# Heads in pairs of nine token slots, and attention in a fixed order among groups of four MLP matmuls

## Chip, cores, metric

The kernel runs on one core of a Trainium2 chip. The metric is the device time of one execution in microseconds (us). A ratio is the record's ratio of fast runs, with its 95% interval; it is not quite the ratio of the medians that are quoted beside it.

Engine names in the profile: PE is TensorE's matmuls, PEld its weight loads, DVE is VectorE, ACT is ScalarE, POOL is GpSimd, SP is SyncE. The granted clock is TensorE's clock as the profile records it, as a share of full speed.

## The reference

Linear ("performer") attention over 64 heads, then an MLP over all 4608 tokens:

```python
# q, k, v: (8, 8, 576, 64); omega: (128, 64)
q_s, k_s = q * scale, k * scale                  # scale = 1 / 64**0.25
phi(x) = exp(x @ omega.T - |x|^2/2 - max(...)) / sqrt(128)
q_p, k_p = phi(q_s), phi(k_s)                    # (8, 8, 576, 128)
kv  = einsum('bhsm,bhsd->bhmd', k_p, v);  z = sum(k_p, axis=s)
out = (q_p @ kv) / (q_p @ z + 1e-6)              # (8, 8, 576, 64)
x = out.transpose(0, 2, 1, 3).reshape(4608, 512)
h = x @ w_in                                     # 512 -> 2048
y = (h * sigmoid(1.702 * h)) @ w_out             # 2048 -> 512
```

The sigmoid is computed as `0.5 * (1 + tanh(0.851 h))`, and the factor 0.5 is applied at the end.

## The kernel before

One head at a time: q and k are transposed together (`qkTp`), projected (`pq`, `pk`), exponentiated on ScalarE, the key maximum is folded into v on VectorE (`maxE`, `emax`, `vp`), `kv` and the numerator and denominator (`nk`) follow, and the quotient goes to `xb`. After eight heads `xb` is transposed into `xt`. The MLP runs over blocks of 512 tokens. The attention is recorded with high priority, and a scheduler decides the order on each engine.

```python
    ps_h = ctx.enter_context(tc.tile_pool(name="ps_h", bufs=2, space=PSUM))   # two rotating buffers
    ps_o = ctx.enter_context(tc.tile_pool(name="ps_o", bufs=1, space=PSUM))
    ...
    def moe_block(tok0, ntok):
        gT = gtp.tile([128, NFC, TOK_BLK], BF16, name="gT", tag="gT")
        for f in range(NFC):                                  # 16 groups of 128 hidden units
            ph = ps_h.tile([128, TOK_BLK], F32, name="ph", tag="ph")
            for c in range(CM):                               # four matmuls: a "first-layer quantum"
                nc.tensor.matmul(ph[:, 0:ntok], lhsT=win[:, c, ...], rhs=xt[c][...],
                                 start=(c == 0), stop=(c == CM - 1))
            th = thp.tile([128, TOK_BLK], BF16, name="th", tag="th")
            nc.scalar.activation(out=th[...], in_=ph[...], func=AF.Tanh, scale=0.851)
            nc.vector.scalar_tensor_tensor(out=gT[:, f, ...], in0=th[...], scalar=1.0,
                                           in1=ph[...], op0=ALU.add, op1=ALU.mult)
        for r0 in range(0, ntok, 128):
            po = ps_o.tile([128, DM], F32, name="po", tag="po")
            for f in range(NFC):                              # 16 matmuls: second layer
                nc.tensor.matmul(po[0:m, :], lhsT=gT[:, f, r0:r0+m], rhs=wout[:, f, :], ...)
            ... osb = 0.5 * po on ScalarE, then stored ...
    ...
    for b in range(B):
        with tc.high_priority(offset=2_000_000):
            for h in range(H):
                attention_head(b, h, xb)
                ...
            xb_to_xt(b, xb)
        ... moe_block for every block whose tokens are there ...
```

The softmax here doesn't subtract the row's maximum and nothing guards it: scores larger than these inputs give would overflow.

## Time and profile before

| | before |
|---|---|
| time, median of 2 | 433.59 us |
| TensorE busy | 86% |
| VectorE busy | 64% |
| DMA packets under 512 B | 124,032 of 132,778 |

The page of the kernel before. First the busy time of each engine with its share of the span and its number of instructions; then, from the strip of 40 equal slices, TensorE and its granted clock in tenths and the DMA share; then the chain of work that ended last, by engine and by line.

```profile
PE 372.1 (86%) x2801; PEld 189.3 (44%) x2801; DVE 276.9 (64%) x787; ACT 208.5 (48%) x454; POOL 139.3 (32%) x345
...
PE   0066597889988899989999899989999999999895
...
PEclk9999999999999999999999999999999999999999
DMA  9999589579799479669879759101101001011011
...
PE 33%; ACT 5%; DVE 4%; issue 1%; DVEq 0%; ACTq 0%
PE po L260 18%; PE ph L237 12%; DVE gT L248 3%; ACT th L245 3%; ACT osb L268 1%; ACT qeT L160 1%; PE qkTp L152 1%; PE nk L200 1%; PE xps L222 0%; PE pq L159 0%; PE nk L188 0%; DVE vp L178 0%; ACT ke L172 0%; DVE xb L209 0%; PE pk L166 0%
```

The reader sees a slow start, then TensorE close to full at full clock to the end. DMA is busy, at first full (share 1.11 in the first 60 us, 0.84 from 80 to 200 us), until shortly before the attention ends at 286 us.

The windows table of the kernel before: per stretch the busy time of each engine with the number of instructions, the granted clock, the DMA share, and GB/s.

```profile
80.00:200.00 120.00, 110.50 (x1005) 58.47 (x1003) 102.92 (x321) 71.26 (x162) 57.80 (x142) 1.00 0.84 93
285.00:420.00 135.00, 129.34 (x613) 57.07 (x612) 49.43 (x88) 51.72 (x95) 0.00 (x0) 1.00 0.10 37
```

While attention runs, VectorE and TensorE are both nearly always busy. In the second line only the MLP is left, but for the last copies of attention up to 286 us, and TensorE is busy 129 of 135 us.

The wait list of the kernel before: who waited for whom, us in total, how often, the longest.

```profile
PE ph L237 <- DVE gT L248: 6.6, 19, 1.4
```

The timeline of the kernel before in that last stage (start, duration, engine, line, what; in brackets the idle time of the engine before it and what ended it). It shows two first-layer quanta in flight:

```profile
397.40 0.38 PE L237 MATMUL ph<-xt_116,win 128*128 128x512 bf16 x1
...
398.27 0.38 PE L237 MATMUL ph<-xt_116,win 128*128 128x512 bf16 x1
398.46 0.60 ACT L245 ACTIVATE th<-ph 128x512 bf16<-128x512 f32 x1 [0.97 <-PE ph L237]
...
399.10 0.69 DVE L248 SCALAR_TENSOR_TENSOR gT<-th,ph 128x512 bf16<-128x512 bf16 x1 [0.88 <-ACT th L245]
...
399.83 0.38 PE L237 MATMUL ph<-xt_116,win 128*128 128x512 bf16 x1
```

A quantum starts at 397.40 and the next one at 398.27, while the first one's tanh (398.46) and gT (399.10) are still to come. The bank of the first (a bank is here one 128x512 float32 buffer of PSUM, the memory that the matmuls write to) is free again at 399.79, and the matmul at 399.83 takes it. So one bank cycles in 2.43 us and carries one quantum; two banks carry two quanta in 2.43 us.

### The profile page before, as it was taken

Reading aid. Unit: us, or ns where it says so; the run is one execution under the profiler, and the core shown is the slowest. Engines: PE = TensorE matmul, PEld = TensorE weight load, DVE = VectorE, ACT = ScalarE, POOL = GpSimd, SP = SyncE. Lnnn points to the kernel's source line nnn. Section 1 sums busy time; section 2 is a strip of 40 time slices with the busy share of each in tenths; the row PEclk is TensorE's granted clock in tenths of the full one; section 3 lists DMA queues with packets and bytes.
Section 4 is the critical chain, followed back from the end, with each engine's and each line's share of the span. In section 5 each row is a group of like instructions: output and inputs, shape, how many; then the busy total and the mean of one; then the engine's idle time right before and its main releaser. Section 6 shows DMA issues by size and latency. Waiting matters only on the chain. (4 is left out here: it accounts for less than half of the span.)

```text
span 431.9 us, 8223 instructions
## 1 busy us (share of the span) xinstructions
PE 372.1 (86%) x2801; PEld 189.3 (44%) x2801; DVE 276.9 (64%) x787; ACT 208.5 (48%) x454; POOL 139.3 (32%) x345
## 2 busy tenths in 40 slices
PE   0066597889988899989999899989999999999895
PEld 0044344454555454445455445444434444444342
DVE  1378769897799878889789878872351441523501
ACT  1044166565576545666467546633452433434412
POOL 8378256256266157256356336000000000000000
PEclk9999999999999999999999999999999999999999
DMA  9999589579799479669879759101101001011011
GB/s 163 248 257 174 63 67 103 66 73 139 120 80 97 70 85 143 93 54 124 130 79 101 81 74 133 38 2 49 50 0 73 27 24 74 1 49 38 7 67 37
DMA packets 132778, 36.21 MB, mean 84 GB/s; under 512 B 124032, under 2 KB 126080, under 8 KB 132736
## 3 DMA queue, kind: packets, MB, share of 16 engines
q0 software_dynamic: 86176, 12.58, 41.5%
q1 hardware_dynamic: 46560, 23.11, 19.4%
q8 instruction: 22, 0.36, 0.4%
q14 instruction: 20, 0.16, 0.1%
HBM read 38.80 MB, written 9.44 MB: 112 GB/s over the span
## 5 line engine op out<-in xcount | busy, mean ns | idle before, releaser
L260 PE MATMUL po<-wout,gT 128*128 128x512 bf16 (+1 forms) x592 | 163.5, 380 | 3.3 <-ACT osb L268 1.8
L248 DVE SCALAR_TENSOR_TENSOR gT<-th,ph 128x512 bf16<-128x512 bf16 (+2 forms) x160 | 99.2, 625 | 93.5 <-ACT th L245 92.8
L245 ACT ACTIVATE th<-ph 128x512 bf16<-128x512 f32 (+2 forms) x160 | 88.4, 555 | 69.1 <-PE ph L237 57.5
L237 PEld LDWEIGHTS <-win 128*128 128x128 bf16 x640 | 56.2, 98 | 58.2 <-issue 13.3
L124 POOL DMA_DIRECT2D qkh<-in_q_dram x63 | 54.7, 868 | 82.0 <-PE qkTp L152 69.6
L260 PEld LDWEIGHTS <-gT 128*128 128x128 bf16 (+1 forms) x592 | 53.7, 98 | 55.2 <-DVE gT L248 5.8
L160 ACT ACTIVATE qeT<-pq 128x512 bf16<-128x512 f32 (+1 forms) x128 | 49.2, 435 | 56.8 <-PE pq L159 43.9
L237 PE MATMUL ph<-xt_116,win 128*128 128x512 bf16 (+2 forms) x160 | 57.2, 360 | 8.4 <-DVE gT L248 6.6
L174 DVE TENSOR_REDUCE maxE<-ke 128x5 f32<-128x640 bf16 x64 | 52.1, 814 | 8.3 <-ACT ke L172 8.1
L237 PE MATMUL ph<-xt_117,win 128*128 128x512 bf16 (+2 forms) x160 | 57.3, 361 | 0.0
L237 PE MATMUL ph<-xt_118,win 128*128 128x512 bf16 (+2 forms) x160 | 57.0, 359 | 0.0
L237 PE MATMUL ph<-xt_119,win 128*128 128x512 bf16 (+2 forms) x160 | 57.0, 359 | 0.0
L128 POOL DMA_DIRECT2D qkh<-in_k_dram x63 | 54.8, 871 | 1.8 <-DMA qkh<-in_k_dram 0.8
L268 ACT ACTIVATE osb<-po 128x512 f32<-128x512 f32 (+1 forms) x37 | 22.1, 598 | 67.6 <-PE po L260 67.6
L159 PE MATMUL pq<-qkT,omT_106 64*128 64x512 bf16 (+1 forms) x128 | 31.8, 320 | 17.5 <-DVE qkT L154 17.3
L172 ACT ACTIVATE ke<-pk 128x640 bf16<-128x640 f32 x64 | 45.6, 712 | 0.3
L152 PE MATMUL qkTp<-ident,qkh 128*128 128x128 bf16 x320 | 31.2, 230 | 12.3 <-DMA qkh<-in_k_dram 5.9
L154 DVE COPY qkT<-qkTp 128x640 bf16<-128x640 bf16 x64 | 30.9, 483 | 12.7 <-PE qkTp L152 11.3
L152 PEld LDWEIGHTS <-qkh 128*128 128x128 bf16 x320 | 24.3, 102 | 33.0 <-issue 28.4
L178 DVE TENSOR_TENSOR vp<-vst,emax 128x325 bf16<-128x325 f32 x64 | 30.6, 478 | 1.4 <-DVE rden L208 0.4
L209 DVE TENSOR_TENSOR xb<-nk,rden 128x320 bf16<-128x320 f32 x64 | 31.0, 484 | 0.3
L166 PE MATMUL pk<-omT_106,qkT 64*128 64x128 bf16 x320 | 31.1, 230 | 0.0
(38 smaller groups left out, 263.1 us busy)
## 6 DMA issues: line engine op xcount, KB each, us to landing
out_dram<-osb SPq DMA_DIRECT2D x35, 256.0 KB, 2.0
vst<-in_v_dram SPq DMA_DIRECT2D x64, 128.0 KB, 2.7
qkh<-in_q_dram POOLq DMA_DIRECT2D x63, 80.0 KB, 3.1
qkh<-in_k_dram POOLq DMA_DIRECT2D x63, 80.0 KB, 3.4
wout_p<-in_moe_w_out_dram SPq DMA_DIRECT2D x16, 256.0 KB, 6.1
win<-in_moe_w_in_dram POOLq DMA_DIRECT2D x16, 128.0 KB, 6.6
vst<-in_v_dram SPq DMA_DIRECT2D x64, 16.0 KB, 2.7
out_dram<-osb SPq DMA_DIRECT2D x2, 128.0 KB, 2.3
```

The costliest lines, as they stand in the source:

```text
L124: nc.gpsimd.dma_start(qkh[:, :, 0:64], qrows[row0 : row0 + SPAD, :].rearrange("(t p) d -> p t d", p=128),)
L128: nc.gpsimd.dma_start(qkh[:, :, 64:128], krows[row0 : row0 + SPAD, :].rearrange("(t p) d -> p t d", p=128),)
L152: nc.tensor.transpose(qkTp[:, t * 128 : (t + 1) * 128], qkh[:, t, :], ident[:])
L159: nc.tensor.matmul(pq[:, 0:cn], lhsT=omT2[0:64, :], rhs=qkT[0:64, c0 : c0 + cn])
L160: nc.scalar.activation(out=qeT[:, c0 : c0 + cn], in_=pq[:, 0:cn], func=AF.Exp, scale=SCALE)
L166: nc.tensor.matmul(pk[:, t, :], lhsT=qkT[64:128, t * 128 : (t + 1) * 128], rhs=omT2[64:128, :],)
L172: nc.scalar.activation(out=ke[:], in_=pk[:], func=AF.Exp, scale=SCALE)
L174: nc.vector.reduce_max(out=maxE[:], in_=ke[:], axis=AX.X)
L237: nc.tensor.matmul(ph[:, 0:ntok], lhsT=win[:, c, f * 128 : (f + 1) * 128], rhs=xt[c][:, tok0 : tok0 + ntok], start=(c == 0), stop=(c == CM ...
L245: nc.scalar.activation(out=th[:, 0:ntok], in_=ph[:, 0:ntok], func=AF.Tanh, scale=0.851)
L248: nc.vector.scalar_tensor_tensor(out=gT[:, f, 0:ntok], in0=th[:, 0:ntok], scalar=1.0, in1=ph[:, 0:ntok], op0=ALU.add, op1=ALU.mult,)
L260: nc.tensor.matmul(po[0:m, :], lhsT=gT[:, f, r0 : r0 + m], rhs=wout[:, f, :], start=(f == 0), stop=(f == NFC - 1),)
```

## The change

Its intent: fewer and larger operations in attention, and a hand-made order that hides them in the MLP.

- Two heads at a time. Each partition holds nine neighbouring tokens of one head (64 partitions per head), read as one contiguous run of 2,304 bytes. Loads and keys are no longer padded to 640 tokens; the query side of the numerator and denominator still is.
- The projections of even and odd slots use the upper and lower half of TensorE's rows ("row-tiled", 64*128 in the trace, where a full one is 128*128), and so do the `kv` matmuls of the two heads.
- The scheduler is switched off. The MLP is cut into 288 quanta of four matmuls: the 16 first-layer quanta of a block, then its 16 second-layer quanta. Attention's steps are placed after fixed quanta, one pair per 8 quanta (per 5 at first). The first four pairs form a prologue.
- gT of a quantum is recorded one quantum late, after the tanh of the next.
- The PSUM buffers become single tiles made once. `ph` is one tile of two banks, used in turn.

```diff
-    ps_h = ctx.enter_context(tc.tile_pool(name="ps_h", bufs=2, space=bass.MemoryType.PSUM))
...
+    with tc.manual_schedule():
...
+        tr = psum.tile([128, 1024], BF16, name="tr")
+        pqk = psum.tile([128, 2, 512], F32, name="pqk")
+        nd = psum.tile([128, 2, 512], F32, name="nd")
+        ph = psum.tile([128, 2, 512], F32, name="ph")
+        po = psum.tile([128, 512], F32, name="po")
...
+        def K(i):                       # key projection of a pair, row-tiled by slot parity e
+            for j in range(4):
+                for e in range(2):
+                    nc.tensor.matmul(pqk[:, e, j*128:(j+1)*128],
+                                     lhsT=t[64*e:64*e+64, j, :], rhs=omT[64*e:64*e+64, :])
+            nc.tensor.matmul(nd[:, 0, 384:512], ...)     # the ninth slot goes to the nd tile
+            nc.tensor.matmul(nd[:, 1, 384:512], ...)
...
+        for i in range(9, npairs):
+            start[i] = start[8] + 8 * (i - 8)
...
+            at(s, t1); at(s + 1, t2); at(s + 2, kk); at(s + 3, ...); ...
...
+        hbanks = [ph[:, 0, :], ph[:, 1, :]]
+        for s, u in enumerate(quanta):
+            if u[0] == "a":                              # first layer
+                dst = hbanks[hb % 2]
+                hb += 1
+                m1(n, f, dst)
+                t = tanh(n, f, dst)
+                for p in pend:
+                    stt(*p)                              # gT of the quantum before
+                pend = [(n, f, t, dst)]
+            else:                                        # second layer
+                m2(n, r, g, po[:])
+                ...
+            for fn in items.pop(s, []):                  # attention steps of this place
+                fn()
```

(The diff is cut to its core and its long lines are shortened.)

## The prediction

> **What bounds it now.** Two stages. Up to 285 us attention runs, and VectorE with its waits bounds it: the windows table gives VectorE 103 of 120 us busy from 80 to 200 us (union; TensorE 110, ScalarE 71). In the timeline at 130-140 us a head takes 3.07 us, with VectorE issuing all the time and six MLP matmuls. From 285 us there is only MLP (TensorE 95%), and the chain of waits is 18% po, 12% ph. Before 57 us little MLP runs and DMA is full (share above 1.0) with 124,032 packets under 512 B.
>
> **What changes.** 32 pairs replace 64 heads, without padding 576 tokens to 640.
> - DMA: 2,304-byte runs in place of 256-byte ones. DMA stops limiting. [...] (share 0.10 for 39 GB/s of 2 KB output packets, 1.1 for 106 GB/s of small ones).
> - VectorE per pair: from the groups, 6.6 us (summed durations) to about 4.6 us: PSUM copy of 1024 about 0.68 (128 takes 0.215, 640 takes 0.483), max halves 0.45, reduce of 576 0.75, vp 0.75, xb 0.81, xt copy 0.45, reciprocals 0.37.
> - ScalarE per pair about equal (3.6 to 3.3 us).
> - TensorE attention about 2.3 us per pair. Row tiling gains little: pq and pk already overlap (135.08 and 135.09 us)[...].
> - MLP: 288 quanta of four matmuls at 0.864 us = 249 us. But order becomes static: a block's first-layer quanta, then its second-layer quanta. Filling ph waits with po goes.
>
> **Critical path, from trace durations.**
> 1. Prologue: four pairs in series, about 9 us each because VectorE and ScalarE are in order: first MLP quantum at about 43 us.
> 2. Block 0 (pairs every 5 quanta): about 49 us.
> 3. Blocks 1-6, a pair per 8 quanta. In first-layer stretches ph has two banks; a bank cycles in 2.43 us (chain: 1.04 matmul, 0.65 tanh, 0.70 gT), so 1.215 us a quantum at best. The large exponential ahead of tanh and the max group ahead of gT stretch 8 quanta with their pair to about 12 us. Second-layer stretches: 8 x 0.864 + 2.3 + po waits, about 10 us. Block: 44 us, six blocks: 264 us.
> 4. Blocks 7-8 without attention: 16 x 1.215 + 4 x 4.30 = 36.6 us each, 73 us.
> 5. Tail 3 us.
> Sum 432 us: most of the saved work turns into static-order waits. I lean lower: the prologue may be pessimistic.
>
> **Prediction: 429 us, range 405 to 450. Faster by over 2%: 0.42; within 2%: 0.36; slower: 0.22.**
>
> **What would show it.** TensorE busy below before's 86%; ph matmuls waiting over 50 us for gT (VectorE); tanh waiting behind exponentials; first MLP matmul at 38-48 us; last two blocks at 36 us each; VectorE busy about 210 us (union); DMA packets under 512 B nearly gone; block period near 44 us; po waiting 0.8 us for osb per output tile at the end.
>
> **What would make it wrong.** Faster: the prologue takes about 25 us, or attention's ScalarE and VectorE work fits between tanh and gT so that a first-layer pair takes 10 us: then about 400. Slower: [...] halved kv matmuls (18 of 65 columns) cost more than 0.03 us each, or late weights stall TensorE's fixed order: then 450 or more.

What no trace or run shows is cut out of it, and each cut is marked. The sum: 43 + 49 + 264 + 73 + 3 = 432 us. TensorE's 2.3 us for a pair is given without its parts and is to be read as an estimate; the other durations are read from the groups and timelines of the kernel before, or estimated from them.

## The result and the profile after

The changed kernel is correct and takes 633.07 us (629.63 and 636.51) against 433.59 us: ratio 1.4603, 95% interval 1.4413 to 1.4793. This is far outside the range of the prediction.

The page after, the same parts: busy time, then TensorE, granted clock and DMA by slices, then the chain, then three of the costliest groups (busy, mean ns of one, idle time of the engine before them and what ended it).

```profile
PE 426.2 (68%) x2834; PEld 195.6 (31%) x2881; DVE 228.1 (36%) x405; ACT 201.4 (32%) x409; POOL 40.6 (6%) x78
...
PE   3456668765886678668865885678658755765575
...
PEclk9999989977798799779978797799789955695569
DMA  9991114411142115111511130002000200020002
...
PE 57%; ACT 20%; DVE 17%; issue 4%; DMA 1%; another core or an unknown queue 1%; POOL 0%; ACTq 0%; DVEq 0%; POOLq 0%
PE ph L253 32%; PE po L273 18%; DVE gT L267 14%; ACT th L263 13%; ACT ke L141 3%; PE nd L215 2%; ACT osb L283 1%; PE pqk L130 1%; PE tr L106 1%; PE tr L238 1%; PE nd L197 1%; DMA qk<-in_q_dram 1%; PE pqk L152 1%; ACT kvs L209 1%; DVE vp L186 1%
...
L253 PE MATMUL ph<-xt,win 128*128 128x512 bf16 x553 | 200.4, 491 | 151.0 <-DVE gT L267 143.1
L267 DVE SCALAR_TENSOR_TENSOR gT<-th,ph 128x512 bf16<-128x512 bf16 x144 | 98.7, 687 | 265.6 <-ACT th L263 265.6
L263 ACT ACTIVATE th<-ph 128x512 bf16<-128x512 f32 x144 | 86.0, 597 | 266.7 <-PE ph L253 263.9
```

VectorE and ScalarE did get less work, and no engine is full. In the chain, ph, th and gT now stand with 32, 13 and 14%. The granted clock also falls, to about half in some slices near the end (0.51 from 501.49 to 540.76 us).

The wait list after, and a line of its windows table for a stretch that has first-layer quanta only (columns as before):

```profile
PE ph L253 <- DVE gT L267: 143.1, 125, 1.8
```

```profile
501.49:540.76 39.27, 22.20 (x48) 6.82 (x49) 8.25 (x12) 7.16 (x12) 0.00 (x0) 0.51 0.00 0
```

TensorE sat idle 143.1 us before first-layer matmuls, waiting for gT, where it had waited 6.6 us. In the stretch of 39.27 us, 12 quanta pass at a granted clock of 0.51, with TensorE busy 22.20 us, VectorE 8.25 and ScalarE 7.16: the three sums make about the whole stretch, which is what one chain through three engines looks like.

The timeline after in a stretch without attention, which is the same work as the stretch shown of before:

```profile
502.87 1.86 PE L253 MATMUL ph<-xt,win 128*128 128x512 bf16 x4 [1.41 <-DVE gT L267]
...
504.77 0.60 ACT L263 ACTIVATE th<-ph 128x512 bf16<-128x512 f32 x1 [2.68 <-PE ph L253]
505.40 0.69 DVE L267 SCALAR_TENSOR_TENSOR gT<-th,ph 128x512 bf16<-128x512 bf16 x1 [2.58 <-ACT th L263]
506.14 0.59 PE L253 MATMUL ph<-xt,win 128*128 128x512 bf16 x1 [1.41 <-DVE gT L267]
```

Matmuls, tanh, gT, matmuls: one at a time, with every engine idle while the two others work. One quantum takes 3.27 us. Two banks are there, but nothing overlaps. The four matmuls take 1.86 us where they took 1.02 us elsewhere (495.57 us, before the clock fell): TensorE also runs at half speed, at the granted clock of 0.51.

At first sight this chain looks impossible, since the next matmuls use the *other* bank. The start of the MLP shows which gT is meant. The timeline after of ScalarE and of VectorE there:

```profile
45.73 0.60 ACT L263 ACTIVATE th<-ph 128x512 bf16<-128x512 f32 x1 [4.97 <-PE ph L253]
48.28 0.60 ACT L263 ACTIVATE th<-ph 128x512 bf16<-128x512 f32 x1 [1.95 <-PE ph L253]
```

```profile
48.91 0.69 DVE L267 SCALAR_TENSOR_TENSOR gT<-th,ph 128x512 bf16<-128x512 bf16 x1 [4.54 <-ACT th L263]
```

The first gT needs the first tanh, which ended at 46.33. VectorE had been idle for 4.54 us, and still gT started only at 48.91, when the *second* tanh had ended. The waits in the built program say the same for quantum 124 of 144:

```
changed kernel:   gT #124 waits for tanh #125     matmuls of #126 wait for gT #124
two tiles (e3):   gT #124 waits for tanh #124     matmuls of #126 wait for gT #124
```

So the theory A that the experiments test: the recording layer treats the tile `ph` as one thing. When different engines use it, it puts all uses in the recorded order, whichever bank they touch. Recorded are matmuls(f), tanh(f), gT(f-1), matmuls(f+1), and that is how they run. The order holds between two *reads* too, and across the banks: tanh #125 and gT #124 read different banks, and gT #124 waits all the same; in the trace the first gT starts at 48.91 us, after the second tanh, and in the two-tile run at 46.37 us, after its own. The waits stand already in the program that the recording layer built; why it sets them is not shown.

### The profile page after: what moved, and what is told of

Read it like the earlier page. It is cut to its first block, busy times and chain, and to the rows that moved or that the text cites. A ratio compares the mean times of both kernels' runs of the same rounds, so it can differ in the third digit from the quotient of the medians.

```text
span 627.9 us, 7057 instructions
## 1 busy us (share of the span) xinstructions
PE 426.2 (68%) x2834; PEld 195.6 (31%) x2881; DVE 228.1 (36%) x405; ACT 201.4 (32%) x409; POOL 40.6 (6%) x78
## 4 chain that ended last, share of the span: by engine, by line
PE 57%; ACT 20%; DVE 17%; issue 4%; DMA 1%; another core or an unknown queue 1%; POOL 0%; ACTq 0%; DVEq 0%; POOLq 0%
PE ph L253 32%; PE po L273 18%; DVE gT L267 14%; ACT th L263 13%; ACT ke L141 3%; PE nd L215 2%; ACT osb L283 1%; PE pqk L130 1%; PE tr L106 1%; PE tr L238 1%; PE nd L197 1%; DMA qk<-in_q_dram 1%; PE pqk L152 1%; ACT kvs L209 1%; DVE vp L186 1%
## 5 line engine op out<-in xcount | busy, mean ns | idle before, releaser
L253 PE MATMUL ph<-xt,win 128*128 128x512 bf16 x553 | 200.4, 491 | 151.0 <-DVE gT L267 143.1
L267 DVE SCALAR_TENSOR_TENSOR gT<-th,ph 128x512 bf16<-128x512 bf16 x144 | 98.7, 687 | 265.6 <-ACT th L263 265.6
L263 ACT ACTIVATE th<-ph 128x512 bf16<-128x512 f32 x144 | 86.0, 597 | 266.7 <-PE ph L253 263.9
L273 PE MATMUL po<-wout,gT 128*128 128x512 bf16 x552 | 142.3, 389 | 8.9 <-ACT osb L283 7.3
L273 PEld LDWEIGHTS <-gT 128*128 128x128 bf16 x576 | 53.6, 100 | 69.1 <-issue 23.1
L169 ACT ACTIVATE qe<-pqk 128x1024 bf16<-128x1024 f32 x28 | 28.6, 1022 | 35.8 <-PE pqk L152 35.8
L83 POOL DMA_DIRECT2D qk<-in_k_dram x32 | 17.1, 536 | 299.3 <-PE tr L121 289.0
L141 ACT ACTIVATE ke<-pqk 128x1024 bf16<-128x1024 f32 x32 | 32.6, 1019 | 1.2 <-PE pqk L130 1.2
L106 PE MATMUL tr<-ident,qk 128*128 128x128 bf16 x256 | 25.5, 256 | 4.5 <-DMA qk<-in_k_dram 1.9
L227 DVE TENSOR_TENSOR xb<-nd,r 128x640 bf16<-128x640 f32 x32 | 26.4, 825 | 1.1
L176 DVE TENSOR_REDUCE m<-hm 128x9 f32<-128x576 bf16 x32 | 24.1, 754 | 1.1
```

The costliest lines, as they stand in the source:

```text
L106: nc.tensor.transpose(tr[:, n * 128 : (n + 1) * 128], qk_t[i][:, j * 128 : (j + 1) * 128], ident[:])
L141: nc.scalar.activation(out=ke[:, 1:9, :].rearrange("p (j e) f -> p e j f", e=2), in_=pqk[:].rearrange("p e (j f) -> p e j f", f=128), func ...
L169: nc.scalar.activation(out=dst, in_=s, func=AF.Exp, scale=SCALE)
L227: nc.vector.tensor_tensor(out=xb[:].rearrange("p g e d -> p e g d"), in0=v4[:, :, :, 0:64], in1=r[:].unsqueeze(3).to_broadcast([128, 2, NG ...
L253: nc.tensor.matmul(dst, lhsT=win[:, c, f * 128 : (f + 1) * 128], rhs=xt[c][:, n * 512 : (n + 1) * 512], start=(c == 0), stop=(c == NC_ - 1),)
L263: nc.scalar.activation(out=t[:], in_=src, func=AF.Tanh, scale=0.851)
```

## The experiments

Four runs test the cause, one more carries it over to the kernel before, and four follow it to a faster kernel. All gave correct results.

### Two lines exchanged

```diff
-                t = tanh(n, f, dst)
                 for p in pend:
                     stt(*p)
+                t = tanh(n, f, dst)
```

> Edit: gT of the quantum before is recorded ahead of tanh of this quantum (two lines change places); the order on each engine stays. Theory A (the two banks of ph are one tile, and all uses of one tile by different engines are put in the recorded order, so that the changed kernel runs matmul, tanh, gT strictly one after another, 2.43 us at full clock and 3.27 us at the low one): now the next matmuls wait for tanh only, so a first-layer quantum takes about 1.04 + 0.65 = 1.7 us at full clock. Blocks 7 and 8 fall from 64 to about 16 x 1.7 + 17.6 = 45 us, the whole to about 480 us (up to 530 if the clock still drops). Rival B (row-tiled matmuls and mode changes, or attention's work in the static order, cost the time): blocks 7 and 8, which hold no attention, and the whole stay as they are, 630 us within 2%. Rival C (my prediction's reading: bank cycle 2.43 us shared by two quanta): no change either, as gT keeps its place on its engine.

Measured: 641.36 us, ratio 1.4797 (1.4767 to 1.4826). The order of instructions on each engine is unchanged. The expected gain did not come, so by numbers this was a miss for A as it was written, and just what rivals B and C had expected (630 us within 2%). The timeline of this run shows which link had been forgotten:

```profile
530.78 1.86 PE L253 MATMUL ph<-xt,win 128*128 128x512 bf16 x4 [1.48 <-ACT th L263]
...
532.75 0.69 DVE L267 SCALAR_TENSOR_TENSOR gT<-th,ph 128x512 bf16<-128x512 bf16 x1 [2.65 <-PE ph L253]
533.47 0.60 ACT L263 ACTIVATE th<-ph 128x512 bf16<-128x512 f32 x1 [2.74 <-DVE gT L267]
534.12 1.86 PE L253 MATMUL ph<-xt,win 128*128 128x512 bf16 x4 [1.48 <-ACT th L263]
```

gT now waits for the *matmuls* of the next quantum, because those are recorded before it and write into the same tile. Then tanh waits for gT. The chain still has three links, in the order in which they are recorded: matmuls, gT, tanh. The built program of this run says the same: gT #124 waits for the matmuls of #125, tanh #125 for gT #124, and the matmuls of #126 for tanh #125. A as I had worded it speaks of all uses, but my number applied it to the readers alone. The run shows that it holds for a write into one bank and a read from the other as well. It also speaks against rival C: one quantum takes 3.34 us here (530.78 to 534.12), and no two share a cycle. Rival B is left to the two-tile run below.

### gT right after its own tanh

```diff
                 t = tanh(n, f, dst)
-                for p in pend:
-                    stt(*p)
-                pend = [(n, f, t, dst)]
+                stt(n, f, t, dst)
```

> Edit: gT is recorded right after its own tanh, no longer one quantum late. ph stays one tile. Theory A: the chain is of the same three links (matmul, tanh, gT, then the next quantum's matmul), so the time stays at about 630 us (within 4%), and a first-layer quantum at 2.43 or 3.27 us. Rival D (only the late recording of gT is at fault, not the tile): the double buffer works again, first-layer quanta without attention take about 1.2 us and the whole falls below 460 us.

Measured: 624.60 us, ratio 1.4410 (1.4381 to 1.4439). As A expected: a quantum without attention takes 3.27 us again (tanh at 508.40 and 511.67). The late recording of gT is not at fault.

### ph as two tiles

```diff
-        ph = psum.tile([128, 2, 512], F32, name="ph")
+        ph = [psum.tile([128, 512], F32, name=f"ph{i}") for i in range(2)]
 ...
-        hbanks = [ph[:, 0, :], ph[:, 1, :]]
+        hbanks = [ph[0][:], ph[1][:]]
```

(The four prologue pairs, which used both banks in one exponential, use two of half the size.)

> Edit: ph becomes two tiles of one bank each (the prologue's query exponential becomes two of half size for it); nothing else. Theory A: gT waits for its own tanh alone, two quanta overlap, a first-layer quantum without attention takes about 1.2 us, blocks 7 and 8 about 36 us each, TensorE stays at full clock, and the whole comes to what my prediction's sum gave, 432 us (415 to 450). Rival B (row tiling, mode changes, attention in static order) says at most the last two blocks gain (55 us), the whole stays above 570 us.

Measured: 441.79 us (441.32 to 442.50), ratio 1.0195 (1.0178 to 1.0212). The same work in the same banks, 191 us less. TensorE stays at full clock (mean 1.000). The timeline of this run, in a stretch without attention:

```profile
380.33 0.60 ACT L263 ACTIVATE th<-ph 128x512 bf16<-128x512 f32 x1 [0.96 <-PE ph L253]
380.96 0.69 DVE L267 SCALAR_TENSOR_TENSOR gT<-th,ph 128x512 bf16<-128x512 bf16 x1 [0.88 <-ACT th L263]
381.20 0.60 ACT L263 ACTIVATE th<-ph 128x512 bf16<-128x512 f32 x1 [0.27 <-PE ph L253]
381.70 1.89 PE L253 MATMUL ph<-xt,win 128*128 128x512 bf16 x8 [0.54 <-DVE gT L267]
...
382.76 0.60 ACT L263 ACTIVATE th<-ph 128x512 bf16<-128x512 f32 x1 [0.97 <-PE ph L253]
```

Two quanta again pass in 2.43 us (380.33 to 382.76). The wait list of TensorE in this run:

```profile
PE ph L253 <- DVE gT L267: 25.3, 62, 1.4
PE nd L215 <- ACT qe L159: 17.1, 27, 0.7
...
PE po L273 <- ACT osb L283: 7.3, 14, 0.7
```

Waits for gT fall from 143.1 to 25.3 us. Rival B, row tiling and the static order, keeps nothing of the 191 us: both are still in this kernel.

### Keeping the wait, filling the idle time

```diff
                 m1(n, f, dst)
+                for _ in range(4):
+                    nc.tensor.matmul(po[:], lhsT=win[:, 0, 0:128], rhs=xt[0][:, 0:512])
                 t = tanh(n, f, dst)
```

> Edit: the changed kernel with four idle matmuls of 512 columns after each first-layer quantum, into the po bank that is unused then (0.86 us of work that nobody reads; the result stays right). The wait stays. Theory A with the clock as its second part (3.27 against 2.43 us is TensorE running at half clock because it idles too much): quanta of 3.27 us become 2.43 us, 58 of 135 measured gaps, so the whole falls by about 45 to 50 us to about 585 us although 123 us of matmul work is added. Rival E (the low clock is a limit on load, not on idleness, or the extra matmuls stand in the chain): no gain or a loss, 630 us or more.

Measured: 584.69 us, ratio 1.3489 (1.3462 to 1.3516); the granted clock of the profiled run reads 1.00 in all slices. Adding 576 useless matmuls made the kernel 48 us *faster*. The timeline of this run:

```profile
526.54 0.60 ACT L263 ACTIVATE th<-ph 128x512 bf16<-128x512 f32 x1 [1.16 <-PE ph L253]
...
527.17 0.69 DVE L267 SCALAR_TENSOR_TENSOR gT<-th,ph 128x512 bf16<-128x512 bf16 x1 [18.55 <-ACT th L263]
527.91 1.02 PE L253 MATMUL ph<-xt,win 128*128 128x512 bf16 x4 [0.55 <-DVE gT L267]
...
528.97 0.60 ACT L263 ACTIVATE th<-ph 128x512 bf16<-128x512 f32 x1 [1.83 <-PE ph L253]
```

The chain is still there (2.43 us a quantum, 526.54 to 528.97), but its matmuls take 1.02 us. So the loss has two parts: about 48 us is the low clock, which goes when TensorE's idle time is filled (mean clock 0.851 in the profiled run of the changed kernel, 1.0 in this one; rival E falls; the 48 us are net of what the idle matmuls themselves cost, which was not measured), and about 143 us (584.7 less 441.8) is the lost overlap at full clock. The traces show both speeds: in the changed kernel, where the granted clock reads 0.51, the weight loads at 503.25, 503.67 and 504.10 us are 0.42 to 0.43 us apart, and in the kernel before, where it reads 1.00, the matmuls at 383.68, 383.90 and 384.11 us 0.21 to 0.22 us.

Short waits came with the low clock: no single wait of ph for gT in the changed kernel was longer than 1.8 us. Three of its quanta with 1.02 us of matmuls in 2.43 us (from 495.57, 498.00 and 500.43 us) ran at full speed, and the next, at 502.87 us, took 1.86 us. With about 1.88 us of matmuls in 2.43 us (the run with idle matmuls, 0.55 us idle) the matmuls stayed at full speed, 1.02 us for four. At which share of idle time the clock falls was not measured.

The record of the clock can also be wrong: between 60 and 80 us the granted clock of the changed kernel reads 1.00 in the windows table, while four matmuls at 62.74 us took 1.87 us, as at the half clock: the weight loads at 63.12, 63.55 and 63.98 us are 0.43 us apart.

### The same declaration in the kernel before

```diff
-    ps_h = ctx.enter_context(tc.tile_pool(name="ps_h", bufs=2, space=bass.MemoryType.PSUM))
+    ps_h = ctx.enter_context(tc.tile_pool(name="ps_h", bufs=1, space=bass.MemoryType.PSUM))
 ...
+    ph2 = ps_h.tile([128, 2, TOK_BLK], F32, name="ph2", tag="ph")
 ...
-            ph = ps_h.tile([128, TOK_BLK], F32, name="ph", tag="ph")
+            ph = ph2[:, f % 2, :]
```

> The kernel before, with its two rotating ph buffers replaced by one tile of two banks, used in turn: only the tile's declaration is changed. Theory A says that one tile is enough to lose the overlap in any kernel: a first-layer quantum waits for gT of the one before. The scheduler can fill part of it with second-layer matmuls and attention. Expected: waits of ph for gT grow from 6.6 us to more than 50 us, a first-layer quantum of the last stage that has nothing between takes 2.43 us or more where two took 2.43 us, and the time rises to 460-500 us. Rival (the loss belongs to the static order of the changed kernel alone): within 2% of 433.6 us.

Measured: 619.66 us, ratio 1.4292 (1.4251 to 1.4334), mean clock 0.827. The wait list of TensorE in this run:

```profile
PE ph L239 <- DVE gT L250: 80.7, 101, 1.2
```

Its timeline in the last block, whose quanta are 448 columns wide, with a second-layer matmul put between:

```profile
521.17 1.65 PE L239 MATMUL ph<-xt,win 128*128 128x448 bf16 x4 [0.86 <-DVE gT L250]
...
522.86 0.54 ACT L247 ACTIVATE th<-ph 128x448 bf16<-128x448 f32 x1 [2.39 <-PE ph L239]
523.43 0.62 DVE L250 SCALAR_TENSOR_TENSOR gT<-th,ph 128x448 bf16<-128x448 bf16 x1 [2.32 <-ACT th L247]
524.11 1.65 PE L239 MATMUL ph<-xt,win 128*128 128x448 bf16 x4 [0.86 <-DVE gT L250]
```

It is the same chain, 2.94 us a quantum. The built programs agree: with one tile the matmuls of quantum 141 wait for gT #140, in the kernel before for gT #139.

The declaration alone costs the old kernel 186 us, with none of the other changes. The scheduler puts second-layer matmuls into the gaps (one at 522.61 us) and cannot hide it. The loss is much larger than I expected (460 to 500 us). The clock falls here too: the waits for gT grow by 74 us (6.6 to 80.7), and the same 2801 matmuls keep TensorE busy 460.6 instead of 372.1 us, at a mean clock of 0.827 instead of 1.000. So neither pairs nor slots nor the static order is needed for the slowdown. Nor is it that the tile is made once instead of rotating: the two tiles above are made once too.

### Small exponentials first

The two-tile kernel still has TensorE waiting 17.1 us for the small exponentials that read `nd`, another tile with several uses. (Here all the uses lie in the same two banks, so this wait is no case of an order across banks.) They were moved ahead of the large one on ScalarE:

```diff
+            nc.scalar.activation(out=ke[:, 0, :], in_=nd[:, 1, 384:512], func=AF.Exp, scale=SCALE)
+            expM(i)
             nc.scalar.activation(out=ke[:, 1:9, :]..., in_=pqk[:]..., func=AF.Exp, scale=SCALE)
-            nc.scalar.activation(out=ke[:, 0, :], in_=nd[:, 1, 384:512], func=AF.Exp, scale=SCALE)
```

> On top of two ph tiles: the two small exponentials that read the nd tile are put ahead of the large one on ScalarE. Theory A's second case: nd too is one tile for several uses, so the output matmuls of the pair before wait for exponentials of the pair now, 17.1 us in 27 waits. Expected: those waits nearly vanish (under 5 us) and the time falls by 8 to 15 us from 442, to 427-434 us. Rival: these waits are off the path (TensorE would wait for gT instead): 442 us within 1%.

Measured: 438.19 us, ratio 1.0106 (1.0080 to 1.0131), 3.6 us better than two tiles (measured in other rounds on another chip, where the kernel before took 433.52 against 433.58 us). The wait list of TensorE in this run:

```profile
PE ph L254 <- DVE gT L268: 37.8, 61, 1.6
...
PE nd L216 <- ACT kvs L210: 4.6, 4, 1.4
```

The wait aimed at is gone, but ph now waits 37.8 us for gT instead of 25.3. Most of the gain turned into another wait of the same engine. The expected 8 to 15 us were missed, and by its number (442 us within 1%) the rival was right.

### Alternating the two layers

```diff
-        for n in range(NBLK):
-            quanta += [("a", n, f) for f in range(NFC)]
-            quanta += [("b", n, r, g) for r in range(4) for g in range(4)]
+        quanta += qa[0] + qb[0] + qa[1]
+        for n in range(1, NBLK - 1):
+            for x, y in zip(qa[n + 1], qb[n]):        # first layer of n+1 with second layer of n
+                quanta += [x, y]
+        quanta += qb[NBLK - 1]
```

with the pairs started earlier. On top of two tiles:

> On top of two ph tiles: the quanta of the second layer of a block alternate with the first-layer quanta of the next block, and the pairs of heads start earlier (4 to 5 quanta apart up to block 2, then 7 to 8). What my prediction named as the cost of the static order (first-layer quanta at 1.2 us or more instead of 0.864, and 0.84 us of po wait per output tile) is filled. Expected: waits of ph for gT below 12 us (25.3 with two tiles), of po for osb below 4 us, the time about 400 us (390 to 415). Rival (TensorE is held by attention's own chain, not by ph and po): above 430 us.

Measured: 411.05 us, ratio 0.9484 (0.9463 to 0.9504). The wait list of TensorE in this run:

```profile
PE ph L253 <- DVE gT L267: 5.4, 10, 1.6
...
PE po L273 <- ACT osb L283: 3.7, 5, 0.9
```

Both waits named in the expectation fall below what it allowed, together by 23.5 of the 30.7 us gained, and the kernel is now faster than before. How much of this the earlier start of the pairs brought was not tested alone.

### Both, and an overlapped prologue

> e6 and e7 together. Expected: the gains add, about 388 us (380 to 402).

Measured: 406.36 us, ratio 0.9376 (0.9353 to 0.9399). The gains do add, but the small exponentials bring 4.7 us here, as they brought 3.6 us alone; the expectation had reckoned with 8 to 15 us of them, and it was missed.

Then the next pair's transposes and copies were recorded ahead of this pair's maxima in the prologue (the edit also gives the large copy of the transposes to VectorE alone, where ScalarE had copied half):

```diff
-        for step in range(7):
-            ... T1, evT1, T2, evT2, K, expK, Q, expQ, then KV, kvs, ND, xm, X, evX of earlier pairs, then mx, vp
+        heads(0)                                       # T1, evT1, T2, evT2
+        for i in range(5):
+            ... K(i), KV(i-1), kvs(i-1), expK(i), Q(i), expQ(i), ND(i-1)
+            heads(i + 1)
+            ... xm(i-1), mx(i), vp(i), X(i-1), evX(i-1)
```

> e8 with the prologue's four pairs overlapped: the next pair's transposes and copies are recorded ahead of this pair's maxima. My prediction put the series at about 9 us a pair, set by in-order VectorE and ScalarE. Expected: first-layer matmuls begin at about 31 us instead of 45, the time 10 to 14 us below e8. Rival: the start is bound by DMA (its share is above 1.0 until 45 us), then no gain.

Measured: 398.82 us, ratio 0.9210 (0.9187 to 0.9233). First-layer matmuls begin at 38.5 us, 6.6 us earlier than in the run before it (45.1), and the time falls by 7.5 us: less than the 14 us and the 10 to 14 us that were expected. Whether DMA, whose share is 1.11 in the first 40 us, or the remaining chain holds it there was not tested. This is the best version: 8% faster than the kernel before.

## Why the prediction was wrong

The stages of the prediction against the traces, in us. Blocks are read from the start of one block's first tanh to that of the next.

| step of the prediction | predicted | after | two tiles |
|---|---|---|---|
| first MLP matmul | 43 | 44.2 | 44.2 |
| block 0 | 49 | 74.6 | 51.7 |
| blocks 1 to 6, each | 44 | 62.4 | 44.7 |
| block 7, without attention | 36.6 | 64.3 | 35.1 |
| an output tile of the second layer, alone | 4.30 | 4.30 | 4.30 |
| sum of the prediction, against the time | 432 | 633.1 | 441.8 |

- **The step that failed is number 3**, "In first-layer stretches ph has two banks; a bank cycles in 2.43 us ... so 1.215 us a quantum at best", and the same 1.215 us in step 4. The bank does cycle in 2.43 us, but in the changed kernel only one bank is in flight, so a quantum without attention takes 2.43 us at full clock and 3.27 us at half clock. Of the 135 gaps between tanh starts within a block, 57 are about 2.43 us and 58 about 3.27 us, and their mean is 2.79 us. I read the banks in the source and took it that the waits would follow them. The waits stand in the built program, which needs no run, and I had not followed gT's wait to the tanh that it names.
- **The second error hung on it**: every duration was taken at full clock. With TensorE busy about 1.02 of 2.43 us, the clock fell, to 0.51 at the lowest stretch shown. This is worth 48 us by the run with idle matmuls.
- **Right**, as the two-tile run shows: the prologue, the length of the blocks, the last blocks and the output tiles: each line of the table is met within 3 us. In the prologue VectorE and ScalarE do run in the recorded order (trace of the changed kernel, 0 to 40 us): ScalarE's first copies for the second, third and fourth pair start at 13.66, 22.18 and 31.12 us, 8.5 and 8.9 us apart (predicted 9). Inside a block of that run (the one from 187.44 us, whose second layer runs from 210.38 to 231.39 us) the 16 first-layer quanta with two pairs take 24.0 us and the 16 second-layer quanta 21.0 us (predicted 24 and 20), so the block is not right by two errors that cancel. With the failed step undone, the prediction's sum is off by 10 us of 442. The reason given, that the saved work turns into waits of the static order, is then also right in kind: two tiles with the static order are about 2% slower than the kernel before, and filling those waits with second-layer matmuls, with the pairs started earlier, gained 31 us (441.8 to 411.1). But the prediction leaned to a faster kernel, and this one is not.
- **Right in the details of cost**: DMA packets under 512 B fell from 124,032 to 2,960. The summed means of VectorE's groups for a pair are 4.3 us (predicted 4.6), of ScalarE's 3.4 us (3.3). Halved kv matmuls are cheap: 18 of them take 0.45 us (at 150.25 us). VectorE was busy 228 us, not about 210. TensorE's busy share fell, to 68%, and ph waited more than 50 us for gT, 143.1 us. But these two signs were also met by a far larger cause than the one I had in mind, so they did not confirm it.
- **A sign that did not come**: "tanh waiting behind exponentials" was not what held tanh. ScalarE was idle 263.9 us before tanh, waiting for ph.
- None of the ways to be slower that the prediction lists (dear kv matmuls, late weights) was the one that came: the kv matmuls took what is quoted above, and TensorE's wait list of the changed kernel has no wait for a weight transfer.

What stays open: whether the whole-tile order was needed for anything. The two-tile runs are correct, so these runs show no need of it for these two banks.

## What to carry to other kernels

In these kernels two banks overlap only if they are two tiles to the layer that sets the waits: 441.8 against 633.1 us here, 433.5 against 619.7 us in the kernel before. When a double buffer is made by slicing one tile, look in the built program at which producer each consumer waits for, or in the trace at an engine that starts when the *wrong* predecessor ends. When three engines take turns with every one of them idle, look for such a chain first. A low clock then comes on top of it as an effect (48 of the 191 us here), so do not take it for the cause. And a removed wait counts only if TensorE does not wait for something else at the same place, as the small exponentials showed: their 17.1 us of waits went, those for gT grew from 25.3 to 37.8 us, and the time fell by 3.6 us.
